# Moving casts, transposes and an upsampling out of the TensorE stream of a fused attention and feed-forward kernel

## The chip, the cores and the metric

The kernel runs on one core of a Trainium2 chip. The metric is the device time of one execution in microseconds (us). Each kernel was run several times, and each experiment ran beside the kernel before on the same chip. All runs that are compared here were fast, that is, within 1.5% of the fastest run of the same kernel. The kernel after was not run again beside the experiments. Ratios are the mean time of one kernel's fast runs over that of the other's fast runs of the same rounds, so they are not quite the ratio of the medians that are quoted beside them.

The engines are called TensorE (PE in the profile, PEld for its weight loads), VectorE (DVE), ScalarE (ACT), GpSimd (POOL) and SyncE (SP).

## The reference, cut to what matters

```python
# q, k, v: (8, 8, 576, 64) float32; factor = 4, scale = 1/8
q_d, k_d, v_d = (t.reshape(B, H, 144, 4, D).mean(axis=3) for t in (q, k, v))
out_up    = np.repeat(softmax(scale * q_d @ k_d.T) @ v_d, 4, axis=2)      # coarse, upsampled
out_local = softmax(where(|i - j| < 4, scale * q @ k.T, -1e9)) @ v        # banded
x = (out_up + out_local).transpose(0, 2, 1, 3).reshape(4608, 512)
y = (maximum(x @ w_gate, 0) * (x @ w_val)) @ w_out                        # 512 -> 1536 -> 512
```

There are 64 heads, handled as 32 pairs: two heads of 64 channels fill 128 partitions. The feed-forward part (FFN) has 4608 tokens, worked on in nine chunks of 512. Of each chunk there are 12 h steps (gate and value, 8 matmuls each) and 4 y steps (12 matmuls each), 1296 matmuls of 128x128 by 512 in all.

## The kernel before

A pair loads q and k as float32 with 96 tokens on the partitions. The casts to fp16 are made by ScalarE and VectorE. TensorE transposes by multiplying with an identity (tp). The rest of the names in the profile follow from the code: sd are the coarse scores, vd is the pooled v, sc the banded scores (a window of 128 keys for each 96 queries), od the coarse output, u the banded output, f the upsampling of od to full length, by a matmul with a 0/1 matrix.

```python
# emit_mid / emit_mid_b: casts, transposes on TensorE, pooling on VectorE
nc.scalar.copy(out=qk16[:, 0, :, 0:64], in_=nat_q[:, 0, :, :])
nc.vector.tensor_copy(out=qk16[:, 1, :, 0:64], in_=nat_k[:, 0, :, :])
nc.vector.tensor_copy(out=vw[:, :, :, 0:64], in_=vst)
...
nc.tensor.matmul(out=tp[:, jj, :], lhsT=qk16[:, ti, 3 * g + jj, :], rhs=I96_sb[:, 0:NQ], ...)
...
# emit_compute: sd head by head, then vd, then sc
for hh in (0, 1):
    for c in range(2):
        nc.tensor.matmul(out=sdp[0:72, c, :],
                         lhsT=k_dT[dlo : dlo + 64, bass.ts(c, 72)], rhs=q_dT[dlo : dlo + 64, :], ...)
for c in range(2):
    for sig in range(3):                                   # vd: 72 stationary columns
        nc.tensor.matmul(out=vd_ps[0:72, c, :, :], lhsT=P72_sb[:, sig, :], rhs=vw[:, :, 3 * c + sig, :], ...)
...                                                        # sc, exp, masks, then od (72 columns)
for j in range(NB):                                        # u: 96 stationary columns
    nc.tensor.matmul(out=up[:, j, :], lhsT=e_sb[hh][j // 3][:, j % 3, :], rhs=vw[:, hh, j, :], ...)
for j in range(NB):                                        # f: upsampling, 96 stationary columns
    nc.tensor.matmul(out=fp[:, j, :], lhsT=E_sb[0:72, j % 3, :], rhs=odn_sb[hh][0:72, j // 3, :], ...)
...                                                        # x_b = u / sum + f, stored to x_dr in DRAM
# before a chunk's h steps: x_dr is read back through a transposing DMA
nc.sync.dma_start(out=t, in_=_dap(x_dr, ...), transpose=True)
```

The FFN weights are loaded as float32, too, and cast by ScalarE. The matmuls of the FFN are spread between those of the attention pairs, so that the long h and y matmuls fill the waits of the short ones.

The softmax here doesn't subtract the row's maximum and nothing guards it: scores larger than these inputs give would overflow.

## Time and profile before

| | before |
|---|---|
| time, median of 6 runs | 441.97 us (440.26 to 442.57) |
| span of the profiled run | 440.0 us |
| TensorE busy | 396.3 us, 90% of the span |
| first FFN matmul | 72.8 us |
| one FFN matmul, back to back | 0.216 us (8 in 1.73 us) |
| one pair on TensorE | 3.07 us |

These are parts 1 and 2 of the profile's page of the kernel before: busy time of each engine, then one digit for each of 40 slices of 11 us (9 is 90% or more busy), the DMA engines' busy share, and what they moved.

```profile
PE 396.3 (90%) x3408; PEld 227.3 (52%) x3408; DVE 298.4 (68%) x812; ACT 211.5 (48%) x485; POOL 7.6 (2%) x100
PE   0217688999999999999999999999999999999996
DVE  0319999998789878977997799769966860330430
DMA  8799989547687777677775646321113112200202
GB/s 292 247 256 259 276 213 248 134 114 177 187 183 171 168 208 174 137 163 216 172 164 129 191 106 138 76 105 32 30 36 109 28 39 48 97 0 10 87 0 95
```

TensorE is at 9 from the eighth slice to the last but one. What is lost is lost before: seven slices, 77 us, with a rising TensorE row and a DMA row at 7 to 9. A change can gain in two places, then: an earlier start of the full stretch, and less TensorE work in it. VectorE is mostly at 7 to 9 there until about 320 us, and has to be watched. The table of stretches says the same in numbers for 165 to 220 us (length, then busy time of PE, PEld, DVE, ACT, POOL, the granted clock, DMA share, GB/s):

```profile
165.00:220.00 55.00, 54.91 (x519) 31.39 (x518) 46.28 (x127) 29.08 (x72) 1.30 (x15) 1.00 0.72 172
```

The view of the tile xT (the FFN's input) shows when the FFN starts, in the words "first and last start":

```profile
L170 PE MATMUL h_ps<-xT,wg_sb x432: 376/379/634, 72.8 to 424.6; 128*128 128x512 f16 x144
```

The timeline of TensorE shows what a pair costs. The columns are the start, the time until the last of the group ends, and the group. As matmuls overlap (the sd group below ends 0.32 us after its start, and vd starts after 0.25), a group's cost is the start of the next group less its own start. (The last group is cut off by the end of the view.)

```profile
219.44 0.32 PE L366 MATMUL sd_ps<-q_dT,k_dT 64*72 64x144 f16 x4
219.69 0.54 PE L377 MATMUL vd_ps<-vwin,p_sb 128*72 128x130 f16 x6
220.16 0.43 PE L405 MATMUL sc_ps<-qT,kT 64*128 64x96 f16 x12
220.61 0.49 PE L429 MATMUL od_ps<-vd_sb,e_d 72*72 72x65 f16 x8
220.94 0.68 PE L319 MATMUL tp_ps<-I_sb,qk 96*128 96x96 f16 x12
221.45 1.03 PE L170 MATMUL h_ps<-xT,wg_sb 128*128 128x512 f16 x4
...
224.91 0.69 PE L463 MATMUL u_ps<-vwin,e_sb 128*96 128x65 f16 x12
225.43 0.70 PE L475 MATMUL f_ps<-odn,E_sb 72*96 72x64 f16 x12
225.97 0.38 PE L170 MATMUL h_ps<-xT,wg_sb 128*128 128x512 f16 x1
```

Read so: sd 0.25, vd 0.47, sc 0.45, od 0.33, tp 0.51, u 0.52, f 0.54 us, together 3.07.

### The profile page before, as it was taken

Reading aid. Unit: us, or ns where it says so; the run is one execution under the profiler, and the core shown is the slowest. Engines: PE = TensorE matmul, PEld = TensorE weight load, DVE = VectorE, ACT = ScalarE, POOL = GpSimd, SP = SyncE. Lnnn points to the kernel's source line nnn. Section 1 sums busy time; section 2 is a strip of 40 time slices with the busy share of each in tenths; the row PEclk is TensorE's granted clock in tenths of the full one; section 3 lists DMA queues with packets and bytes.
Section 4 is the critical chain, followed back from the end, with each engine's and each line's share of the span. In section 5 each row is a group of like instructions: output and inputs, shape, how many; then the busy total and the mean of one; then the engine's idle time right before and its main releaser. Section 6 shows DMA issues by size and latency. Waiting matters only on the chain.

```text
span 440.0 us, 9037 instructions
## 1 busy us (share of the span) xinstructions
PE 396.3 (90%) x3408; PEld 227.3 (52%) x3408; DVE 298.4 (68%) x812; ACT 211.5 (48%) x485; POOL 7.6 (2%) x100
## 2 busy tenths in 40 slices
PE   0217688999999999999999999999999999999996
PEld 0116575555555555655565556555655654444442
DVE  0319999998789878977997799769966860330430
ACT  2435976564565455545564556445633532332331
POOL 0000000000000000000000000000000000000000
PEclk9999999999999999999999999999999999999999
DMA  8799989547687777677775646321113112200202
GB/s 292 247 256 259 276 213 248 134 114 177 187 183 171 168 208 174 137 163 216 172 164 129 191 106 138 76 105 32 30 36 109 28 39 48 97 0 10 87 0 95
DMA packets 171730, 60.64 MB, mean 138 GB/s; under 512 B 164264, under 2 KB 164520, under 8 KB 171688
## 3 DMA queue, kind: packets, MB, share of 16 engines
q1 hardware_dynamic: 164008, 41.21, 42.1%
q10 hardware_dynamic: 7680, 18.88, 11.6%
q8 instruction: 26, 0.43, 0.4%
q14 instruction: 16, 0.13, 0.1%
HBM read 41.20 MB, written 14.16 MB: 126 GB/s over the span
## 4 chain that ended last, share of the span: by engine, by line
PE 80%; DMA 10%; DVE 4%; SPq 3%; ACT 1%; issue 1%; DVEq 0%; ACTq 0%
PE h_ps L170 21%; PE h_ps L175 21%; PE y_ps L191 19%; DMA vst<-in_v_dram 5%; PE tp_ps L319 3%; PE od_ps L429 3%; PE f_ps L475 3%; PE u_ps L463 3%; PE vd_ps L377 3%; SPq L292 2%; PE sc_ps L405 2%; DMA nat<-in_k_dram 2%; PE sd_ps L366 2%; DMA out_dram<-y_sb 1%; DMA wstage<-in_moe_w_out_dram 1%; DMA masks_sb<-band_masks 1%
## 5 line engine op out<-in xcount | busy, mean ns | idle before, releaser
L182 DVE TENSOR_TENSOR gT<-r,h_ps 128x512 f16<-128x512 f16 x108 | 73.4, 682 | 61.7 <-PE h_ps L175 61.1
L180 ACT ACTIVATE r<-h_ps 128x512 f16<-128x512 f32 x108 | 64.9, 601 | 104.0 <-PE h_ps L170 95.8
L170 PE MATMUL h_ps<-xT,wg_sb 128*128 128x512 f16 x432 | 111.8, 381 | 0.0
L175 PE MATMUL h_ps<-xT,wv_sb 128*128 128x512 f16 x432 | 110.9, 379 | 0.0
L191 PE MATMUL y_ps<-wo_sb,gT 128*128 128x512 f16 x432 | 95.7, 379 | 0.0
L175 PEld LDWEIGHTS <-wv_sb 128*128 128x128 f16 x432 | 42.3, 98 | 51.3 <-issue 0.6
L191 PEld LDWEIGHTS <-gT 128*128 128x128 f16 x432 | 41.6, 98 | 48.2
L170 PEld LDWEIGHTS <-wg_sb 128*128 128x128 f16 x432 | 40.2, 99 | 41.8 <-issue 0.6
L195 ACT COPY y_sb<-y_ps 128x512 f32<-128x512 f32 x36 | 21.1, 586 | 78.9 <-PE y_ps L191 72.9
L415 ACT ACTIVATE e_sb<-sc_ps 128x288 f16<-128x288 f32 x128 | 42.0, 416 | 1.1 <-PE sc_ps L405 1.1
L319 PE MATMUL tp_ps<-I_sb,qk 96*128 96x96 f16 x384 | 27.4, 222 | 14.1 <-ACT qk L302 10.3
L418 DVE TENSOR_TENSOR e_sb<-e_sb,masks_sb 128x288 f16<-128x288 f16 x128 | 36.3, 300 | 4.9 <-ACT e_sb L415 4.9
L486 DVE TENSOR_TENSOR t<-u_ps,rdu 96x384 f16<-96x384 f32 x64 | 32.4, 545 | 0.0
L492 DVE TENSOR_TENSOR x_b<-t,f_ps 96x384 f16<-96x384 f16 x64 | 32.3, 542 | 0.0
L463 PEld LDWEIGHTS <-e_sb 128*96 128x96 f16 x384 | 24.8, 138 | 11.5 <-DVE e_sb L418 6.0
L389 ACT ACTIVATE e_d<-sd_ps 72x288 f16<-72x288 f32 x64 | 22.5, 402 | 16.9 <-PE sd_ps L366 16.8
L463 PE MATMUL u_ps<-vwin,e_sb 128*96 128x65 f16 x384 | 25.3, 220 | 5.7 <-DVE e_sb L418 5.7
L394 DVE CAST vd_sb<-vd_ps 72x130 f16<-72x130 f32 x64 | 15.6, 284 | 20.0 <-PE vd_ps L377 20.0
L429 PE MATMUL od_ps<-vd_sb,e_d 72*72 72x65 f16 x256 | 18.4, 206 | 12.0 <-ACT e_d L389 5.7
L319 PEld LDWEIGHTS <-qk 96*128 96x128 f16 x384 | 21.4, 107 | 14.4 <-ACT qk L302 10.3
L330 DVE CAST kT<-tp_ps 128x288 f16<-128x288 f32 x64 | 26.7, 441 | 1.5 <-PE tp_ps L319 1.5
L303 DVE CAST qk<-nat 96x384 f16<-96x384 f32 x32 | 11.2, 349 | 23.8 <-DMA nat<-in_k_dram 23.8
(30 smaller groups left out, 338.5 us busy)
## 6 DMA issues: line engine op xcount, KB each, us to landing
vst<-in_v_dram SPq DMA_DIRECT2D x62, 192.0 KB
nat<-in_q_dram SPq DMA_DIRECT2D x32, 288.0 KB
nat<-in_k_dram SPq DMA_DIRECT2D x32, 288.0 KB
out_dram<-y_sb ACTq DMA_DIRECT2D x8, 1024.0 KB
x_dr<-x_b SPq DMA_DIRECT2D x32, 144.0 KB
wstage<-in_moe_w_gate_dram ACTq DMA_DIRECT2D x4, 768.0 KB
wstage<-in_moe_w_val_dram ACTq DMA_DIRECT2D x4, 768.0 KB
wstage<-in_moe_w_out_dram ACTq DMA_DIRECT2D x12, 256.0 KB
```

What stands on the lines that cost most here:

```text
L170: nc.tensor.matmul(out=h1, lhsT=wg_sb[:, kk, bass.ts(jj, 128)], rhs=xts[kk], start=(kk == 0), stop=(kk == 3),)
L175: nc.tensor.matmul(out=h2, lhsT=wv_sb[:, kk, bass.ts(jj, 128)], rhs=xts[kk], start=(kk == 0), stop=(kk == 3),)
L180: nc.scalar.activation(out=r1, in_=h1, func=AF.Relu)
L182: nc.vector.tensor_tensor(out=gt, in0=r1, in1=h2, op=ALU.mult)
L191: nc.tensor.matmul(out=y_ps, lhsT=st["gts"][jj][:, bass.ts(ty, 128)], rhs=wo_sb[:, jj, :], start=(jj == 0), stop=(jj == NJJ - 1),)
L319: nc.tensor.matmul(out=tp[:, jj, :], lhsT=qk16[:, ti, 3 * g + jj, :], rhs=I96_sb[:, 0:NQ], start=True, stop=True,)
L415: nc.scalar.activation(out=esb, in_=scps[hh][:, :, 0:NQ], func=AF.Exp, scale=scale)
L418: nc.vector.tensor_tensor(out=esb, in0=esb, in1=masks_sb[:, 3 * g2 : 3 * g2 + 3, :], op=ALU.mult,)
L429: nc.tensor.matmul(out=od_ps[0:72, hh, tcx, :], lhsT=ed_sb[hh][:, c, bass.ts(tcx, 72)], rhs=vd_sb[hh][:, c, :], start=(c == 0), stop=(c == 1),
L463: nc.tensor.matmul(out=up[:, j, :], lhsT=e_sb[hh][j // 3][:, j % 3, :], rhs=vw[:, hh, j, :], start=True, stop=True,)
L486: nc.vector.tensor_tensor(out=t2, in0=u_ps[hh][:, :, 0:64], in1=_sap(rdu, (0, 96), 0, [[1, 6], [0, 64]]), op=ALU.mult,)
L492: nc.vector.tensor_tensor(out=x_b[:, :, bass.ts(h0 + hh, 64)], in0=t2, in1=f_ps[hh], op=ALU.add,)
```

## The change

The intent is to leave TensorE nothing but matmuls that need it, and to start the FFN earlier. The kernel is nearly written anew. These are the parts that matter:

```diff
-nc.sync.dma_start(nt, ...)             # float32, then casts by ScalarE and VectorE
+nc.gpsimd.dma_start(dst[:, :, 64 * hh : 64 * hh + 64],          # the DMA casts to fp16
+    _dap(src, off + hh * S * D, [[D, 96], [NQ * D, NB], [1, D]]))   # 576 pieces of 256 bytes
 (v and the three weights likewise)

+NPE = 12, LEAD = 6
 # transposes of q and k
-TensorE (tp) in all 32 pairs
+if hp < NPE:  TensorE (tp), copied out by ScalarE
+else:         nc.sync.dma_start_transpose(out=qT[r3]..., in_=q16[r]...)

 # stationary operands
-lhsT=P72_sb[:, sig, :]      (72 columns)        +lhsT=pool_sb[:, sig, :]              (128, zero-padded)
-lhsT=ed_sb[hh][.., 72]      (72 columns)        +lhsT=ed[r2][:, hh, s0 : s0 + 128]    (128)
-lhsT=e_sb[..]               (96 columns)        +lhsT=ee[r2][:, hh, 96 * j : 96 * j + 128]  (128)

 # sd
-for hh: for c: matmul(...)                      +for c: for hh: matmul(...)
 # vd
-between sd and sc                               +later, between two h steps

 # upsampling and x
-f matmuls; x_b = u / sum + f; store to DRAM; transposing DMA back
+xo = [u / sum | od / sum]; nc.sync.dma_start_transpose(out=xoT[r2], in_=xo)   # on chip
+xT[...] = xoT[:, 0:6] + broadcast(xoT[:, 6:8])    # one VectorE add, [96, 2], [1, 72], [0, 4]

-order of instructions by the scheduler
+written order on TensorE and VectorE; at step s: pair s+6, three h steps and one y step
+the weight slices: gate and value at s = -4 .. -1, one quarter of w_out at s = 0, 1, 2, 3
```

## The prediction

> **What bounds the kernel now.** TensorE. In the table of stretches it is busy 54.9 of every 55 us from 110 to 385 us, at granted clock 1.00; VectorE is busy 43 to 47 there until 330 us, DMA 0.2 to 0.76. Time is lost at the start: up to 77 us TensorE is busy only 38 us, DMA share is 0.74 to 1.04, and the first FFN matmul (view of tile xT) starts at 72.8 us.
>
> From the timeline (200 to 226 us): an FFN matmul takes 0.216 us back to back (8 in 1.73), so 1296 cost 280 us. A head pair costs 2.01 us (sd 0.25, vd 0.47, sc 0.45, od 0.33, tp 0.51) plus 1.06 (u 0.52, f 0.54) = 3.07; 32 cost 98. Sum 378 of 440 us.
>
> **What the change does to TensorE.**
> - The upsampling matmuls f go (-0.54 per pair): the DMA transpose of x carries the coarse result along, and one VectorE add broadcasts it.
> - 20 of 32 pairs lose the tp matmuls (-0.51): q and k are transposed by DMA.
> - od, u and vd get stationary operands of 128 columns instead of 72 or 96. [...] weight loads of 128 columns take 98 to 107 ns, of 96 columns 138; tp (128 columns, 96 moving) runs at 42 ns per matmul, f (96 columns, 64 moving) at 45. Estimate by moving columns: u 43 to 30 ns, od 41 to 30, vd 78 to 57, together -0.38 per pair.
>
> A pair then costs 2.15 us (first 12) or 1.64: 59 in total, 39 us less, all on the critical path.
>
> **Other engines.** Casts of q, k, v and the weights move into DMAs issued by GpSimd. Per steady step (3 h, 1 y, one pair: 9.4 us of TensorE) I sum VectorE from traced durations: pooling 1.48, masks 1.2, gT 2.05, u and od scaling with reciprocals 2.2, vd about 0.4, add about 0.65: 8.0 us. ScalarE about 5. So TensorE stays the bound. In the steps with tp the pooling comes late: about 1 us stall in each of six, 6 us.
>
> **The start.** The FFN begins after six pairs; seven pairs (6.9 MB) and the first weight slices (1.6 MB) precede it. At the 250 GB/s traced in the first 77 us that is 34 us plus about 5 us latency; six steps of about 6 us VectorE work plus a first load give about the same. I take 50 us instead of 73.
>
> **Sum.** 50 + 280 + 46 (the remaining 26 pairs) + 6 + 3 (last copy and store) = 385 us span, about 386 us time. Range 368 to 415. Chances: faster 0.90, same 0.05, slower 0.05.
>
> **What would show it.** First h matmul near 50 us; TensorE over 97% busy afterwards; u near 30 ns per matmul; no f; weight loads of u and od near 100 ns; total TensorE work near 339 us; VectorE near 85% in the middle.
>
> **What would make it wrong.** Descriptor generation on GpSimd: each pair needs 3840 pieces of 256 B read and 128 B written, and no trace here shows its rate. If a pair took over 9.4 us, loads would set the pace (waits on q, k, v tiles) and the kernel could be slower. VectorE now runs in written order, so one late DMA transpose holds all behind it; eight PSUM banks in rotation could add stalls. A slow start costs one for one.

The 0.38 us per pair is an estimate, roughly scaled by moving columns from the 42 ns that tp takes with 96 of them. The "about 5 us latency" has no source in the text; in the kernel after, the loads of q, k and v take a median of 5.8, 5.2 and 5.3 us from issue to landing. What the text calls descriptor generation shows there as busy time of GpSimd: 0.75 us for a transfer of 576 pieces, 0.86 us for one of 768.

## The result and the profile after

| | before | after |
|---|---|---|
| time, median | 441.59 us (440.26 to 443.7, 16 runs) | 393.09 us (392.12 to 393.8, 8 runs) |
| ratio | | 0.8903, 95% interval 0.8886 to 0.8921 |
| span of the profiled run | 440.0 us | 391.4 us |
| first FFN matmul | 72.8 us | 49.7 us |
| one pair on TensorE in the full stretch | 3.07 us | 1.48 us, with tp 1.99 |
| TensorE busy | 396.3 us | 351.4 us |

Parts 1 and 2 of the page of the kernel after (slices of 9.8 us):

```profile
PE 351.4 (90%) x2784; PEld 185.3 (47%) x2784; DVE 241.9 (62%) x588; ACT 163.0 (42%) x385; POOL 159.7 (41%) x229
PE   1647499874999999999999999999999999999996
DVE  1487878870887777777777777777765532223220
POOL 9999657687666755455553431120000000000000
DMA  7999999999999999999999997862112200010012
GB/s 66 106 130 159 166 159 169 145 165 136 145 162 151 165 176 184 131 131 138 138 139 115 142 137 101 107 102 65 49 47 63 59 28 27 28 54 27 28 42 94
```

The TensorE row reaches 9 in the sixth slice already, at 49 us, falls to 8, 7 and 4 in the eighth to tenth (68 to 98 us), and is at 9 from the eleventh on. The DMA row stays at 9 until the 24th slice, far longer than before. The GB/s row must not be compared with the one of before: the page counts the casting queue at 20.47 MB while 41.16 MB were read from memory, so it counts what is written, which is half of what is read. The view of xT in the kernel after:

```profile
L328 PE MATMUL h_ps<-xT,wg_sb x432: 377/379/634, 49.7 to 376.0; 128*128 128x512 f16 x144
```

The FFN starts 23.1 us earlier. The same stretch of 55 us as above:

```profile
165.00:220.00 55.00, 55.00 (x463) 28.48 (x462) 42.33 (x104) 25.59 (x60) 27.31 (x36) 1.00 1.48 135
```

TensorE is busy for all of it, VectorE for 42.33 us of 55 (77%), GpSimd for 27.31 us, all of it issue of DMAs. (A DMA share above 1 stands as the table gives it; nothing here rests on it.) One steady step on TensorE:

```profile
223.94 0.32 PE L219 MATMUL sd_ps<-qd,kd 64*72 64x144 f16 x4
224.09 0.42 PE L234 MATMUL sc_ps<-qT,kT 64*128 64x96 f16 x12
224.44 2.76 PE L344 MATMUL y_ps<-wo_sb,gT 128*128 128x512 f16 x12
...
228.77 0.41 PE L270 MATMUL od_ps<-vd,ed 72*128 72x65 f16 x8
229.01 0.55 PE L282 MATMUL u_ps<-vw,ee 128*128 128x65 f16 x12
229.40 1.03 PE L328 MATMUL h_ps<-xT,wg_sb 128*128 128x512 f16 x4
...
231.13 0.51 PE L204 MATMUL vd_ps<-vw,pool_sb 128*128 128x130 f16 x6
231.48 1.02 PE L328 MATMUL h_ps<-xT,wg_sb 128*128 128x512 f16 x4
...
233.30 0.32 PE L219 MATMUL sd_ps<-qd,kd 64*72 64x144 f16 x4
```

The step takes 9.36 us from sd to sd. In it sd is 0.15 us, sc 0.35, od 0.24, u 0.39, vd 0.35, together 1.48 us. The 36 FFN matmuls and a gap of 0.1 us between the last h matmuls and sd take the remaining 7.88 us, 0.219 for each matmul with the gap, 0.216 without it.

Between 49.7 and 110 us TensorE waits. The two longest waits, in the timeline (the bracket gives the idle time before the group, and what ended it):

```profile
86.93 0.81 PE L344 MATMUL y_ps<-wo_sb,gT 128*128 128x512 f16 x3 [1.95 <-DMA wo_sb<-in_moe_w_out_dram]
93.21 1.44 PE L344 MATMUL y_ps<-wo_sb,gT 128*128 128x512 f16 x3 [5.47 <-DMA wo_sb<-in_moe_w_out_dram]
94.44 1.90 PE L328 MATMUL h_ps<-xT,wg_sb 128*128 128x512 f16 x4
```

The first y steps need the output weights, which have not landed. The longer wait costs more than its 5.47 us: the seven matmuls after it (93.21 to 96.15 us) take 2.94 us, where seven at 0.216 us take 1.51. Between 90 and 96 us the profile records a granted clock of 0.50, and 1.00 again from 97 on. Further waits are 2.3 us in four pieces around the tp matmuls of pairs 8 and 9 (62 to 73 us), most of it for the loads of q and k, and 0.39 us for a pooled k.

With these readings the difference of the spans, 48.6 us, can be split up:

| part | how it is worked out | us |
|---|---|---|
| earlier start of the FFN | 72.8 - 49.7 | 23.1 |
| f gone | 0.54 x 26 pairs after the start | 14.0 |
| tp gone | 0.51 x 20 pairs | 10.2 |
| u and od | (0.13 + 0.09) x 26 | 5.7 |
| sd, vd and sc | (0.10 + 0.12 + 0.10) x 26 | 8.3 |
| new waits | 1.95 + 5.47 + 2.3 + 0.39 | -10.1 |
| rest | 1.7 of it slow matmuls: the seven after the wait 1.4; the first eight of the FFN 2.81 us, in the kernel before 2.58, later 1.73 in both | -2.6 |

The number 26 is an estimate of how many pairs lie after the start; it is right to about one pair. Which row is due to what is the subject of the experiments.

### The profile page after: what moved, and what is told of

Read it like the earlier page. It is cut to its first block, busy times and chain, and to the rows that moved or that the text cites. A ratio compares the mean times of both kernels' runs of the same rounds, so it can differ in the third digit from the quotient of the medians.

```text
span 391.4 us, 7480 instructions
## 1 busy us (share of the span) xinstructions
PE 351.4 (90%) x2784; PEld 185.3 (47%) x2784; DVE 241.9 (62%) x588; ACT 163.0 (42%) x385; POOL 159.7 (41%) x229
## 3 DMA queue, kind: packets, MB, share of 16 engines
q0 software_dynamic: 133584, 20.47, 78.6%
HBM read 41.16 MB, written 9.44 MB: 129 GB/s over the span
## 4 chain that ended last, share of the span: by engine, by line
PE 75%; DMA 11%; POOL 9%; DVE 2%; issue 1%; ACT 0%; POOLq 0%; DVEq 0%
PE h_ps L328 43%; PE y_ps L344 24%; DMA q<-in_q_dram 5%; DMA wv_sb<-in_moe_w_val_dram 5%; POOL vw L162 3%; POOL q L131 2%; PE u_ps L282 2%; POOL k L131 2%; PE vd_ps L204 2%; DMA wo_sb<-in_moe_w_out_dram 2%; PE od_ps L270 1%; PE sd_ps L219 1%; PE sc_ps L234 1%; DVE gT L338 1%; POOL vw L139 0%
## 5 line engine op out<-in xcount | busy, mean ns | idle before, releaser
L131 POOL DMA_DIRECT2D q<-in_q_dram x64 | 47.7, 760 | 50.2 <-DMA qT<-q 41.2
L162 POOL DMA_DIRECT2D vw<-in_v_dram x62 | 52.3, 862 | 33.7 <-PE u_ps L282 26.4
L131 POOL DMA_DIRECT2D k<-in_k_dram x64 | 47.0, 749 | 9.9 <-DMA vw<-in_v_dram 3.4
L251 ACT ACTIVATE ee<-sc_ps 128x288 f16<-128x288 f32 x128 | 41.5, 413 | 0.0
L254 DVE TENSOR_TENSOR ee<-ee,masks_sb 128x288 f16<-128x288 f16 x128 | 36.5, 307 | 7.6 <-ACT ee L251 7.4
L301 DVE TENSOR_TENSOR xo<-u_ps,ru 96x384 f16<-96x384 f32 x64 | 35.4, 554 | 2.2
L242 ACT ACTIVATE ed<-sd_ps 72x288 f16<-72x288 f32 x64 | 22.6, 402 | 29.6 <-PE sd_ps L219 29.6
L195 DVE TENSOR_REDUCE qd<-qT 128x144 f16<-128x576 f16 x32 | 23.8, 744 | 9.2 <-ACT qT L178 9.2
L312 DVE TENSOR_TENSOR xT<-xoT 128x576 f16<-128x576 f16 x32 | 24.0, 751 | 1.8 <-DMA xoT<-xo 1.8
L195 DVE TENSOR_REDUCE kd<-kT 128x144 f16<-128x576 f16 x32 | 23.8, 743 | 1.8 <-ACT kT L178 1.8
```

The costliest lines, as they stand in the source:

```text
L131: nc.gpsimd.dma_start(dst[:, :, 64 * hh : 64 * hh + 64], _dap(src, off + hh * S * D, [[D, 96], [NQ * D, NB], [1, D]]),)
L162: nc.gpsimd.dma_start(t[:, hh, :, 0:64], _dap(v, base + hh * S * D, [[D, 128], [NQ * D, NB], [1, D]]),)
L195: nc.vector.tensor_reduce(out=dst, in_=src.rearrange("p (t f) -> p t f", f=4), axis=AX.X, op=ALU.add)
L251: nc.scalar.activation(out=o, in_=sc_ps[g][hh].rearrange("p j t -> p (j t)"), func=AF.Exp, scale=scale)
L254: nc.vector.tensor_tensor(out=o, in0=o, in1=masks_sb[:, 3 * g : 3 * g + 3, :].rearrange("p j t -> p (j t)"), op=ALU.mult,)
L301: nc.vector.tensor_tensor(out=x[:, 0:NB, 64 * hh : 64 * hh + 64], in0=us[hh][0:96, :, 0:64], in1=_sap(ru, (0, 96), 0, [[1, NB], [0, 64]]), ...
```

## The experiments

The theory: the kernel is bound by TensorE in both versions, so it gains what its TensorE stream loses, in the form of f, tp, wider stationary operands and an earlier start; and the early part loses 10 us to new waits. The rivals: VectorE or GpSimd is the limit instead; the gain of the small matmuls comes from something other than width; the waits on the output weights are an accident of order or else a sign that loading limits the whole early part.

### Transposes back to TensorE (e1)

```diff
-    NPE = 12
+    NPE = 32
```

> The changed kernel with q and k of all 32 pairs transposed by matmuls (the DMA transposes of the last 20 pairs undone). Theory (TensorE work sets the pace once the FFN has begun): 20 pairs x 0.51 us of tp matmuls = 10 us slower than the changed kernel's 393, plus up to 0.4 us per step where pooling comes late (the changed kernel lost 0.39 us so in its fourth FFN step): 403 to 411 us. Rival (the gain came from the new order of work and from relieving VectorE and ScalarE; TensorE work has slack): within 3 us of 393, or slower only by waits on ScalarE copies that the waits view would show.

Measured: 407.92 us, ratio 0.9247 (0.9221 to 0.9273), 14.8 us above the kernel after. A steady step grew from 9.36 to 10.08 us (222.72 to 232.80). That is 0.72 us for 20 steps, 14.4 us. The tp matmuls account for 0.51 of it; the remaining 0.21 is the pooling, which now follows the transposes so late that sd comes after a larger gap (VectorE ends the pooled k at 232.75 us, sd starts at 232.80). Moving the transposes of 20 pairs to the DMA is worth 14 to 15 us, as expected.

### The width of the stationary operands (e2 and e4)

In the kernel after, the operands are made as narrow as they were:

```diff
-lhsT=pool_sb[:, sig, :]                     +lhsT=pool_sb[:, sig, 0:72]
-lhsT=ed[r2][:, hh, s0 : s0 + 128]           +lhsT=ed[r2][:, hh, s0 : s0 + 72]
-lhsT=ee[r2][:, hh, NQ * j : NQ * j + 128]   +lhsT=ee[r2][:, hh, NQ * j : NQ * j + 96]
```

> The changed kernel with the stationary operands of vd, od and u narrowed back to 72, 72 and 96 columns; nothing else. Theory (the width decides the rate): per pair u 12 x (43-32.5 ns), od 8 x (41-30 ns), vd 6 x (78-58 ns) = 0.34 us, times the 26 pairs that run beside the FFN = 9 us slower, about 402 us, with the weight loads of u back from 103 to about 138 ns. Rival (order of work, not width): same time within 2 us, the matmuls keep 32, 30 and 58 ns.

Measured: 397.17 us, ratio 0.9004 (0.8973 to 0.9035). It is 4.1 us above the kernel after, half of what was expected. Three groups of its timeline, in order of time:

```profile
223.33 0.51 PE L204 MATMUL vd_ps<-vw,pool_sb 128*72 128x130 f16 x6
...
230.33 0.44 PE L270 MATMUL od_ps<-vd,ed 72*72 72x65 f16 x8
230.61 0.70 PE L282 MATMUL u_ps<-vw,ee 128*96 128x65 f16 x12
...
232.88 0.51 PE L204 MATMUL vd_ps<-vw,pool_sb 128*72 128x130 f16 x6
```

The step from vd to vd takes 9.55 us, 0.19 more than with 128 columns. The timeline gives u 0.54 us instead of 0.39, and od 0.28 instead of 0.24. The costliest groups, with the mean ns of one, show the weight loads of u, first with 96 columns (this experiment), then with 128 (the kernel after):

```profile
L282 PEld LDWEIGHTS <-ee 128*96 128x96 f16 x384 | 22.5, 137 | 0.0
```

```profile
L282 PEld LDWEIGHTS <-ee 128*128 128x128 f16 x384 | 15.9, 103 | 0.0
```

That is what the prediction said of u. The weight loads of vd, too, take 105 ns with 128 columns, and 124 with 72. But vd takes 0.35 us with 72 columns and with 128, 58 ns for each matmul; why, no run shows. The width of vd buys nothing.

The other way round, the kernel before got 128 columns for vd, od, u and f, padded with zeros:

```diff
-P72 = np.zeros((128, 3, 72), np.float16)    +P72 = np.zeros((128, 3, 128), np.float16)
-E72 = np.zeros((128, 3, 96), np.float16)    +E72 = np.zeros((128, 3, 128), np.float16)
 (e_d and e_sb become slices of rings that are 64 and 32 columns longer, zeroed once)
```

> The kernel before with one part of the change alone: stationary operands of vd, od, u and f widened with zeros to 128 columns. Theory: f 45 to about 32 ns, u 43 to 32.5, od 41 to 30, vd 78 to 58 = 0.49 us per pair, 26 pairs beside the FFN: 13 us faster, about 429 us. Rival (the gain needs the new schedule): same time within 2 us as 441.6.

Measured: 432.33 us, ratio 0.9797 (0.9771 to 0.9824), so 8.3 us saved against 13 expected. In its timeline u takes 0.39 us and f 0.35 (29 ns for one, 45 before), while vd still takes 0.45 and od 0.32, as good as before. The two experiments agree for u, f and vd: width is worth 0.13 to 0.15 us per pair for u, another 0.19 for f where there is an f, and nothing to 0.02 for vd. For od it is worth 0.04 in the new kernel and at most 0.01 in the old one; the rest of od's 0.09 in the change stays open. The 0.12 us that vd gained in the change must come from elsewhere.

### The order of the small matmuls (e9)

In the last 20 pairs of the kernel after, sd is issued head by head and vd stands between sd and sc, as before. Widths stay at 128.

```diff
-for c in range(2): for hh in range(2):      +for hh in range(2): for c in range(2):   # hp >= NPE
     sd matmul
+if hp >= NPE: emit_vd(hp)
 sc matmuls
```

> The changed kernel, but in the last 20 pairs TensorE works in the order of the kernel before: sd head by head instead of alternating heads, then vd, then sc; operands, widths and everything else unchanged. The narrow run showed vd at 58 ns with 72 columns as well, and the widened kernel before still had vd at 75 ns, so the width didn't explain vd. Theory (switching between matmuls of 64 rows and of 128 rows costs about 0.1 us each, and alternating heads halves sd): sd 0.15 to 0.25 us, vd 0.35 to 0.47, sc 0.35 to 0.45, that is 0.3 us per pair, 6 us in all, 397 to 400 us. Rival (something else in the new kernel, such as the weight loads of kd): within 2 us of 393.

Measured: 399.32 us, ratio 0.9052 (0.9006 to 0.9098), 6.2 us above the kernel after. The timeline of TensorE in one of these pairs:

```profile
227.92 0.32 PE L222 MATMUL sd_ps<-qd,kd 64*72 64x144 f16 x4
228.17 0.52 PE L204 MATMUL vd_ps<-vw,pool_sb 128*128 128x130 f16 x6
228.63 0.43 PE L239 MATMUL sc_ps<-qT,kT 64*128 64x96 f16 x12
```

Here sd takes 0.25 us again instead of 0.15, and vd 0.46 instead of 0.35; sc, 0.36, hardly moves. The step is 9.58 us, 0.22 longer, which makes 4.4 us over 20 pairs of the 6.2 measured; the other 1.8 are not assigned. So the order explains what width didn't in vd and sd.

Two things were undone together, the order of the heads in sd and the place of vd. The timeline tells them apart. Cut into windows of a nanosecond, it shows the four sd matmuls of both kernels starting at 0, 0.01, 0.09 and 0.10 us from the first. What differs is the next group: sc follows 0.15 us after the first sd matmul in the kernel after, and vd 0.25 us in this experiment. The theory also put a part of sd's time down to the order of the heads; the equal starts speak against it here. What is left is the place of vd. sd and sc stand in the timeline with 64 rows (64*72 and 64*128), vd, h and y with 128. With vd in between, there are two changes more of the number of rows in each pair, and each comes with about 0.1 us: sd to vd 0.25 instead of sd to sc 0.15, and vd to sc 0.46 instead of vd to h 0.35. A third such change stands in both kernels, from h to sd: the eight h matmuls before sd take 1.82 us, those before od or vd 1.73. The runs show these intervals; what happens within them they don't.

The 0.10 us that sc gained in the change stays open. It didn't return with the old order, nor with the old widths (e2: 0.35), and it wasn't there to be had by width in the kernel before (e4: 0.45). There, od follows sc at once.

### The upsampling matmuls (e5)

The kernel before, without its f matmuls; the second operand of the add is the first one again. Its output is wrong, which doesn't matter for the time.

```diff
-        f_ps = ...  12 matmuls with E_sb
-                in1=f_ps[hh],
+                in1=t2,
```

> The kernel before without its upsampling matmuls f; the VectorE add that read them adds its first input to itself instead (wrong result on purpose, same number of VectorE instructions). Theory (f is 0.54 us of TensorE per pair on the critical path of the 26 pairs beside the FFN): 14 us faster, about 427 us. Rival (removing f paid only because it also took work from VectorE and changed the order): within 3 us of 441.

Measured: 424.52 us, ratio 0.9625 (0.958 to 0.967), 16.4 us saved. The first h matmul comes at 67.6 us instead of 72.8, so some 5 us of it come from the start and 11 from the full stretch, where the table above has 14.0. A step with four h steps takes 9.54 us from sd to sd, instead of 10.02 to 10.08. The traced cost of f, 0.54 us per pair, was a fair measure of its worth.

### Is VectorE close to being the limit? (e6)

One more VectorE reduction of 0.74 us in each of 20 steady steps:

```diff
+if 6 <= s < 26:
+    nc.vector.tensor_reduce(out=dmy, in_=xT[:, 0, 0:576]..., axis=AX.X, op=ALU.max)
```

> The changed kernel with one more VectorE reduction (128x576, about 0.74 us, result not used) in each of the 20 steady steps. Theory (TensorE is the bound, VectorE is idle about 1.5 us of each 9.36 us step): at most 3 us slower than 393. Rival (VectorE in written order is as critical, so relieving it was a part of the gain): 15 us slower.

Measured: 394.87 us, ratio 0.8958 (0.8909 to 0.9006). 14.8 us of work added 1.8 us to the median, and the intervals of the two kernels overlap. The step is still 9.36 us, TensorE is busy 55.00 of 55 us, VectorE 46.2 to 46.5. VectorE is not the limit of the steady step.

### The output weights earlier (e3)

```diff
-elif s < 4: emit_wo(s)
+elif s == 0: emit_wo(0)
+elif s == 1: emit_wo(1); emit_wo(2); emit_wo(3)
```

> The changed kernel with the four loads of the output weights asked for earlier in the GpSimd queue: all before the head-pair loads 11 and 12 instead of one after each of loads 9 to 12. Theory (what the prediction missed is the wait of 7.4 us for the output weights at 85 to 93 us, because they queue behind pair loads that are not needed yet): 7 to 9 us faster, 384 to 386 us, no wait of y matmuls on the weights of over 1 us. Rival (the ramp is simply limited by what the DMA engines can move): the wait moves to the q and k tiles, gain under 3 us.

Measured: 390.62 us, ratio 0.8862 (0.8831 to 0.8893): 2.5 us gained by the medians, 1.8 by the ratios, whose intervals overlap, where 7 to 9 were expected. Of the wait on the output weights 1.04 us was left. But another wait came up at 100 us, here in the timeline of VectorE:

```profile
100.75 0.76 DVE L312 TENSOR_TENSOR xT<-xoT 128x576 f16<-128x576 f16 x1 [6.00 <-DMA xoT<-xo]
```

VectorE waited 6.00 us for the transpose of x, and TensorE's h matmuls 2.04 us at 104 us for VectorE's gT. That transpose stands in SyncE's queue behind those of q and k of the next pairs, whose loads had been pushed back by the weights. VectorE works in written order, so gT came late. As in the kernel after, a slow stretch followed the wait: TensorE's matmuls from 104.36 to 112.25 us took about 3.5 us more than in a steady step, and from 106 to 110 us the recorded clock is 0.50. The loads that have to come by then had only been put in another order. This is the rival theory, that loading limits the early part, and the run speaks for it. It doesn't show it: the place of the transposes in SyncE's queue, the same in the kernel after, was not changed by itself.

### Pooling by TensorE in the first twelve pairs (e7)

The transposing matmul gets 24 further columns that sum four tokens each, so the pooled q and k come out of it, and VectorE's two reductions (0.74 us each) go:

```diff
-eye_sb: [96, 96] identity
+eye_sb: [96, 120], columns 96..119: sums of four
-emit_pool(hp + 1)
+nc.scalar.copy(out=dd[:, 72 * g : 72 * g + 72]..., in_=tp[:, :, NQ:120])
```

> The changed kernel with the pooled q and k of the first 12 pairs made by the transposing matmul (24 more columns in its moving operand) and copied by ScalarE, in place of two VectorE reductions of 0.74 us per pair. Theory (each of the six steps before the FFN takes 6.5 us because VectorE is busy 5.9 us of it): steps of about 5 us, first h matmul at 41 to 44 us instead of 49.7. End to end then either 5 to 8 us faster (if the start alone counts) or under 3 us faster (if the ramp up to the first y is limited by what DMA can move, so that the time reappears as a longer wait for the output weights).

Measured: 391.91 us, ratio 0.8891 (0.8846 to 0.8936), 1.2 us better in the median, with intervals that overlap. Of the two outcomes named it is the second, a gain under 3 us. The steps before the FFN shrank from 6.5 us to between 4.0 and 5.5 us, once the first pair was through. Then TensorE waited for data:

```profile
43.53 0.76 PE L180 MATMUL tp_ps<-eye_sb,q 96*128 96x120 f16 x6 [5.43 <-DMA q<-in_q_dram]
...
91.20 1.44 PE L355 MATMUL y_ps<-wo_sb,gT 128*128 128x512 f16 x3 [3.96 <-DMA wo_sb<-in_moe_w_out_dram]
```

The first h matmul came at 47.1 us, 2.6 us earlier, not at 41 to 44, and the last slice of the output weights let y go on at 91.20 us, 2 us earlier than in the kernel after. Take VectorE away as the limit of the early steps, and loading is there at once. The waits on the output weights are as long as before, 7.4 us in all; the time came back in the wait for q. That q had been asked for by GpSimd at 33.03 us, ten microseconds before it landed, and between 38.6 and 43.4 us GpSimd itself waited 3.4 us for transfers in flight: here it was the transfer that was late, and not its issue. By the time that y goes on in the kernel after, 13 pairs of 0.98 MB (v is read in overlapping windows) and 9.4 MB of weights have been loaded, 22.2 MB in 93 us, or about 240 GB/s. The prediction took 250 GB/s, but counted only what precedes the first h matmul.

### Longer pieces (e10, e11, e12)

If loading is the limit, loading in longer pieces may help. That a piece costs time beyond that of its bytes, no run here measures by itself. In e10 q and k of the first twelve pairs are read in runs of six rows, 1536 bytes, so that six consecutive tokens lie in one partition. The transposing matmuls are then made one per row and head, and ScalarE's copy puts the tokens in order:

```diff
-_dap(src, off + hh * S * D, [[D, 96], [NQ * D, NB], [1, D]])
+_dap(src, off, [[NB * D, 96], [S * D, 2], [1, NB * D]])
-nc.scalar.copy(out=dst[:, 288 * g : 288 * g + 288], in_=tp...)
+nc.scalar.copy(out=dst.rearrange("c (p r) -> c r p", r=NB)[:, 3 * g : 3 * g + 3, :], in_=tp)
```

> The changed kernel with q and k of the first 12 pairs read in runs of six rows (1536 B into 768 B, both heads in one DMA: 192 pieces instead of 1152 for q, the same for k); TensorE transposes per head (24 matmuls of 64 columns in place of 12 of 128) and ScalarE writes the columns back in token order. Theory (up to 93 us the many small pieces limit what the DMA engines deliver, and that sets when the output weights arrive): waits of y on the weights under 2 us instead of 7.4, no waits on q and k in the FFN, 8 to 10 us less, minus up to 3 us for the extra transposing matmuls: 384 to 388 us. Rival (bytes, not pieces, limit the ramp): the waits stay and the time is 393 to 396 us.

Measured: 405.65 us, ratio 0.9205 (0.9156 to 0.9254). This is a miss: slower by 12.6 us, where a gain was expected. No wait on the output weights is left: the first y starts at 101.27 us without one. That is 18 us later than in the kernel after, but GpSimd had issued the last of the four loads by 61.2 us, against 87.2, so the weights did come sooner. But the first h matmul comes only at 59.1 us, and sd waits 2.7 to 4.3 us in each step for the pooled k. The groups of ScalarE show the reason, in this experiment first, then in the kernel after:

```profile
L189 ACT CAST kT<-tp_ps 128x288 f16<-128x288 f32 x24 | 27.5, 1341 | 0.0
```

```profile
L178 ACT CAST kT<-tp_ps 128x288 f16<-128x288 f32 x24 | 8.6, 416 | 2.0 <-PE tp_ps L174 1.9
```

The copy writes two bytes out of every twelve, and takes three times as long. For k it is 1341 ns instead of 416, for q 1236 instead of 402.

Two variants took the first pairs off this path. In e11 pairs 0 to 4 keep the short pieces and get the pooling of e7, and only pairs 5 to 11 get long pieces; e12 is e11 with the output weights as early as in e3.

```diff
-if hp < NPE:  long pieces
+if NPP <= hp < NPE:  long pieces          # NPP = 5
+if hp < NPP:  short pieces, pooling by the transposing matmul
```

> The same with long runs for pairs 5 to 11 only, and the pooling of pairs 0 to 4 done by the transposing matmul as in the run before. If pieces limit the ramp, the start can now move as well: first h matmul at 41 to 45 us, 379 to 385 us in all. If bytes limit it, the time stays at 390 to 393 us.

> The same again with the output weights asked for before the loads of pairs 11 and 12. If pieces limit the ramp, this adds little to the run before (0 to 3 us); if bytes do, it gives the 2.5 us that it gave alone.

Measured: 396.92 us (0.8998, 0.8959 to 0.9036) and 395.27 us (0.8957, 0.8909 to 0.9005). Both missed for the same reason, so that neither separates pieces from bytes; the 1.7 us between them lie within their intervals. In e11 sd waited 21.8 us in seven pieces for the pooled k, behind the slow copies, and no y waited for weights.

### Pieces of three rows (e13)

The stride can be moved from ScalarE's write to TensorE's: with three consecutive tokens in a partition, each matmul writes every third column of its output tile, and the copy is contiguous on both sides. Otherwise it is e11.

```diff
-_dap(src, off, [[NB * D, 96], [S * D, 2], [1, NB * D]])
+_dap(src, off, [[3 * D, 96], [288 * D, 4], [1, 3 * D]])      # 768 bytes
-out=tp[64 * hh : 64 * hh + 64, jj, :]
+out=tp[64 * hh : 64 * hh + 64, :, jj]                         # tp is [128, 96, 3]
-nc.scalar.copy(out=dst.rearrange("c (p r) -> c r p", r=NB)[...], in_=tp)
+nc.scalar.copy(out=dst[:, 288 * g : 288 * g + 288], in_=tp...)
```

> As e11_long_and_pool, but pairs 5 to 11 are read in runs of three rows (768 bytes read, 384 written) so that three consecutive tokens lie in one partition; the transposing matmuls, one per row and head, write the three-token stride into PSUM (12 bytes) and the ScalarE copy is contiguous on both sides. Theory A (e10 to e12 lost their gain only to the ScalarE copy with a 12-byte write stride, 1.24 to 1.34 us instead of 0.41): the copies fall back to 0.40 to 0.45 us, no y matmul waits for the output weights, the first h matmul comes at 42 to 46 us, and the run takes 378 to 387 us. Theory B (the short loads were never the limit of the ramp, or the strided PSUM write moves the cost to TensorE): 390 us or more, with either the wait on the output weights back or the 12 transposing matmuls of one q or k well over 0.6 us.

Measured: 388.7 us (386.63 to 390.33), ratio 0.8815 (0.8769 to 0.8861). It is the fastest of the correct kernels, about 1% below the kernel after, and yet 1.7 us above the range of theory A. The copies are back at 401 to 413 ns, and the first h matmul comes at 46.4 us, just outside the 42 to 46 of theory A. Two things of B came true in part. The transposing matmuls got slower; here they are in this experiment, and then in e10, where the same matmuls write to PSUM contiguously:

```profile
76.31 0.69 PE L187 MATMUL tp_ps<-eye_sb,q 96*64 96x96 f16 x12
76.79 0.70 PE L187 MATMUL tp_ps<-eye_sb,k 96*64 96x96 f16 x12
77.43 1.04 PE L364 MATMUL h_ps<-xT,wg_sb 128*128 128x512 f16 x4
```

```profile
75.08 0.45 PE L184 MATMUL tp_ps<-eye_sb,q 96*64 96x96 f16 x12
75.36 0.42 PE L184 MATMUL tp_ps<-eye_sb,k 96*64 96x96 f16 x12
75.71 1.04 PE L353 MATMUL h_ps<-xT,wg_sb 128*128 128x512 f16 x4
```

The 24 matmuls take 1.12 us with the stride and 0.63 without, 1.8 times as long, and for seven pairs 3.4 us more. And the wait on the output weights is back, 0.28 and 4.70 us; the longer one in the timeline of this experiment:

```profile
87.02 1.44 PE L380 MATMUL y_ps<-wo_sb,gT 128*128 128x512 f16 x3 [4.70 <-DMA wo_sb<-in_moe_w_out_dram]
```

As everything is earlier, the fourth quarter of the weights, which GpSimd issues only at 79.85 us in the written order, lands after 7 us in a pipeline that wants it at 82. The slow stretch after this wait, 87.02 to 93.77 us, costs another 2.9 us by the same reckoning as above. Here the time of issue is to blame and not the bytes. e13 with the order of e3 would be the next kernel to try; it was not run.

## Why the prediction was right or wrong

The prediction was 386 us with a range of 368 to 415, and faster by over 2% at 0.90. The kernel took 393.09 us and is faster by 11%. Its sum was 50 + 280 + 46 + 6 + 3 = 385 us of span. The trace gives 49.7 + 283.7 (1296 at 0.219, the gaps before sd included) + 41.5 (20 pairs at 1.48 and 6 at 1.99) + 10.1 (waits) + 4.2 (from the start of the last matmul) = 389.2, and 2.2 more, about what the slow matmuls at the start of the FFN and after the longer wait cost (1.1 and 1.4 us). That the total came within 2% owes something to luck: the pairs were put 4.5 us too dear and the late pooling about 5 us too dear, which hid most of the 10.1 us of waits that were missed.

- **TensorE stays the bound: right.** It is busy 55.00 of 55 us from 110 to 330 us, and 14.8 us of further VectorE work added 1.8 to the median (e6). VectorE was put at 85%; it is at 77%. "TensorE over 97% busy afterwards" holds from 110 us on (98.6% to the end), not between 49.7 and 110, where it is busy 83%.
- **The start at 50 us instead of 73: right, 49.7.** Both limits that were named, VectorE's steps of about 6 us (6.5 in the trace) and loading, are there: with the first lifted, the second stopped the FFN from starting before 47.1 us (e7). The 39 us for loading were too few: in e7 about 7.8 MB (pairs 0 to 5, the first weight slices and the q of pair 6) had been asked for up to the q that landed at 43.5 us, an estimated 180 GB/s where 250 was taken.
- **f and tp: right.** e5 gave 16.4 us for f, and e1 14.8 for the tp of 20 pairs, against sums of 17.3 (0.54 x 32) and 10.2 (0.51 x 20). The additional 4 us of e1 are pooling that comes late.
- **Wider operands, 0.38 us per pair: mis-sized.** The step that failed is the estimate by moving columns for all three groups. u and od gain 0.22 in the timeline, 0.19 by e2, 0.14 by e4. vd gains nothing or next to nothing from width (0.35 us at both widths in e2, 0.45 instead of 0.47 in e4).
- **The place of vd: not foreseen.** sd and vd gain 0.22 us per pair by vd not standing between two groups of 64 rows (e9). It made up for the error about vd. With it, and with the 0.10 us of sc that stays open, the pair came out at 1.48 us where 1.64 was predicted. The sum was nearly right with a wrong reason in it; without e9 the trace would have seemed to confirm it.
- **The late pooling in the steps with tp, 6 us: too large.** In these steps the gap before sd is 0.10 to 0.31 us, where every step has 0.1, and one wait of 0.39 us was recorded.
- **The waits between 60 and 95 us, 10.1 us: missed.** This is the step that cost the most. The prediction counted the bytes that precede the first h matmul. It did not ask what has to come during the first chunk: the output weights and six further pairs. Loading, about 240 GB/s up to 93 us, kept TensorE waiting until then and not only until 50.
- **GpSimd's issue of DMAs, named as what could go wrong: not in the steady steps, open in the early part.** A q or k transfer of 576 pieces takes GpSimd 0.75 us and a v transfer of 768 pieces 0.86 us (192 pieces took 0.65 to 0.68 us in e10, 384 mostly 0.67 to 0.68 in e13), so 4.7 us per pair against a step of 9.36 us. GpSimd's row stands at 9 in the first four slices, close to a limit in the early steps of 6.5 us; in e7 the transfers were what TensorE waited for at 43.5 us. For the wait at 93 us it may be otherwise: from 72.84 to 92.0 us GpSimd is busy for all but 1.8 us, and it comes to the fourth quarter of the output weights only late:

```profile
86.44 0.76 POOL L365 DMA_DIRECT2D wo_sb<-in_moe_w_out_dram  x1
```

The quarter landed 6.8 us later, the median of these loads. So the time at which GpSimd gets to issue is a rival to what the DMA engines can move; no run separates the two there, and longer pieces (e10 to e13) relieve both.

## What to carry to other kernels

When an engine is busy for whole stretches, the traced cost of a group on that engine (start of the next group less its own start) was a good price for removing it here (f: 17.3 us by the trace, 16.4 measured in e5); but the cost of a small matmul depended on its neighbours (four sd matmuls: 0.15 us before sc, 0.25 before vd), so where order and shape changed together, each should be tested alone. When a change moves the start of the steady part forward, count the bytes that must have landed at each later point, not just at the start: the next wait is a load that used to have slack, and a wait can cost more than its length, as the slow matmuls after it show (seven in 2.94 us instead of 1.51). And when pieces of a transfer are made longer, look at which engine pays for the stride that this leaves behind (ScalarE 1341 ns instead of 416 in e10, TensorE 1.12 us instead of 0.63 in e13).
